# Attention and a gated feed-forward layer on one core: three score banks as one PSUM tile, one maximum pass over two banks, and eight bias rows on ScalarE

## The chip, the cores and the metric

The kernel runs on one core of one Trainium2 chip. The metric is the device time of one execution in microseconds (us); a time stands for the median of its runs. The engines are TensorE (PE, with its weight loads PEld), VectorE (DVE), ScalarE (ACT), GpSimd (POOL), and SyncE (SP), which issues most of the DMAs.

## What is computed

```python
def _attn_ref(q, k, v, s):                    # q, k, v: 8 x 8 x 576 x 64, s: 8 x 8 x 576
    scores = scale * np.matmul(q, k.transpose(0, 1, 3, 2))
    causal = np.triu(np.ones((S, S), dtype=bool), k=1)
    cum = np.cumsum(np.maximum(s, 0.0), axis=-1)
    bias = -(cum[:, :, :, None] - cum[:, :, None, :])
    scores = np.where(causal, -1000000000.0, scores + np.minimum(bias, 0.0))
    scores = scores - np.max(scores, axis=-1, keepdims=True)
    attn = np.exp(scores)
    attn = attn / (np.sum(attn, axis=-1, keepdims=True) + 1e-09)
    return np.matmul(attn, v).astype(np.float32)

def _moe_ref(x, w_gate, w_val, w_out):        # x: 4608 x 512, d_ff = 1536
    gate = 1.0 / (1.0 + np.exp(-(x @ w_gate)))
    val = x @ w_val
    return (gate * val @ w_out).astype(np.float32)
```

The attention's output, with its heads side by side, is the x of the feed-forward part. The bias of a score is a row term, which a softmax takes no notice of, and a column term, the cumulated s; so the kernel adds one row of 576 values per head to all score rows.

## The kernel before

There are 64 heads, numbered through: batch 0 has heads 0 to 7, batch 1 heads 8 to 15. The 576 query rows of a head are cut into five tiles (`TILES`): tile 0 has 64 rows and 64 columns, tile t of 1 to 4 has 128 rows and 64 + 128 t columns, so the longest, tile 4, has 576 columns and the others 448, 320, 192 and 64. A head's tiles are done from 4 down to 0, one in each tick of the main loop, five ticks a head.

A tile goes through these steps. PE makes its scores in PSUM (`n_s` for batch 0 in fp32, `s_part` from head 8 on with operands split into fp16 high and low parts, lines 446 and 447). A PSUM bank holds 512 fp32 values of a partition, so tile 4 is made in two pieces of 288 columns in two banks. GpSimd masks the diagonal block of the bias row in place (`mask_part`, line 461). VectorE adds the bias row to the scores, writes the sum to SBUF and takes the row's extreme in the same instruction (`n_max`, line 584, and `max_part`, line 471), followed by a short instruction that reads the accumulator out. For tile 4 there are two such pairs, and the second starts from the first's result `em`. ScalarE then takes the exponential with that extreme as its bias (lines 587 and 474). The bias row `rl` of a head from 8 on is the head's cumulated row `cr`, spread over all partitions by GpSimd, times a factor of the pair of heads in `qkcf`; `bias_row` makes it on VectorE (line 455). Batch 0 takes the row as it is.

The score pieces take PSUM banks in turn: `score_bank` hands out two buffers of the tag "s" and one of the tag "x", every third piece the latter. A head has six pieces, so tile 4 always lies in the two "s" banks, tile 3 in "x", tiles 2 and 1 in the "s" banks and tile 0 in "x".

Behind the exponentials, `p_part` splits the probabilities into two fp16 parts, DMAs transpose them (`pt`), `av_part` multiplies them with v on PE, and `split_x` and another DMA put the pair's columns into x. The feed-forward part runs in groups of 256 rows: `ffn_in` (line 657, PSUM tile `gv`) has 24 matmuls for each of 12 slices of the hidden width, `ffn_mid` splits the hidden values (lines 672 and 673), `ffn_out` (line 687, PSUM tile `o`) has 6 matmuls of 512 columns a slice. One such slice of a group is called a unit. Groups 0 and 1, 24 units, need the x of batch 0 alone and start while batch 1's attention runs; group 2 needs rows of batch 1. Weights come in as fp32 and are split on ScalarE and VectorE during the first 12 heads.

The order of each engine's queue is not the order of the code: a scheduler lays it out when the kernel is built, by the dependencies, by priorities (`tc.high_priority` in `first`) and by its own estimate of when things are ready. A new PSUM buffer is handed out when the last reader of the old one is done. So an edit can move instructions everywhere.

## Time and profile before

| | before |
|---|---|
| median of 3 runs | 1154.72 us (1151.44 to 1156.39) |
| span of the profiled execution, first to last instruction | 1146.4 us |
| PE busy | 1091.6 us |
| VectorE busy | 776.1 us |
| ScalarE busy | 749.5 us |
| mean granted TensorE clock | 0.985 |

The profile is one execution, taken by itself. It begins with its first and ends with its last instruction; what a run's time has beyond that span is not in it. A row for a group of instructions names the line, the engine, the operation and the tiles (output <- inputs, without buffer numbers), then shapes, the count, the busy time in us, the mean duration of one in ns, and the engine's idle time ahead of them with what ended it. A row of the windows gives, for a stretch of the span, busy us and instruction counts by engine, the granted clock of TensorE, the mean busy share of the 16 DMA engines, and GB/s. In the rows of the slices a digit is the busy share of a fortieth of the span in tenths. A timeline row begins with start and duration in us.

### The profile page before, as it was taken

How to read it: one execution, taken by the hardware profiler on the slowest of the kernel's cores; microseconds unless marked ns; L12 is line 12 of the kernel's file. 1: busy time of each engine (PE TensorE's matmuls, PEld its weight loads, DVE VectorE, ACT ScalarE, POOL GpSimd, SP SyncE). 2: the span in 40 equal slices, each digit the busy share in tenths (PEclk: the TensorE clock that was granted, in tenths of full speed). 3: DMA queues.
4: the chain of work that ended last, by engine and by line, in shares of the span. 5: the costliest groups of instructions: out<-in, count | busy, mean ns of one | idle time of the engine just before them, and what ended most of it. 6: DMA issues, size and time to landing. Idle time of an engine off the chain costs nothing.

```text
span 1146.4 us, 30336 instructions
## 1 busy us (share of the span) xinstructions
PE 1091.6 (95%) x11644; PEld 853.5 (74%) x11644; DVE 776.1 (68%) x2395; ACT 749.5 (65%) x1465; POOL 261.3 (23%) x568
## 2 busy tenths in 40 slices
PE   6787888989999999999999999999999999999998
PEld 4566676658767887788777777778877887787775
DVE  6899999866787777776565677777777775222222
ACT  6989778667777777676665577767776764233222
POOL 6634233222232222121211122212222221000000
PEclk9889899999999999999999999999999999999999
DMA  9676868995989888777646498868887774000000
GB/s 280 201 217 161 185 139 181 183 189 130 171 164 175 164 178 167 141 150 138 145 79 139 89 178 166 166 144 171 156 161 138 150 124 88 13 20 20 1 19 19
DMA packets 445518, 157.62 MB, mean 137 GB/s; under 512 B 403583, under 2 KB 435839, under 8 KB 445374
## 3 DMA queue, kind: packets, MB, share of 16 engines
q1 hardware_dynamic: 418686, 127.38, 57.6%
q10 hardware_dynamic: 23328, 17.04, 4.9%
q0 software_dynamic: 3360, 11.27, 3.0%
q8 instruction: 91, 1.49, 0.5%
q14 instruction: 53, 0.43, 0.1%
HBM read 56.92 MB, written 9.58 MB: 58 GB/s over the span
## 4 chain that ended last, share of the span: by engine, by line
PE 76%; DMA 7%; DVE 5%; issue 5%; ACT 5%; SPq 1%; POOL 1%; ACTq 0%; DVEq 0%; POOLq 0%
PE gv L657 42%; PE o L687 22%; PE s L447 3%; PE s L446 3%; DMA qk<-in_q_dram 1%; PE av L506 1%; PE av L508 1%; PE av L507 1%; DMA v<-in_v_dram 1%; DVE e L471 1%; PE s L575 1%; DMA pt<-p 1%; DMA T<-T 1%; PE na_ps L605 1%; DMA nqk<-in_q_dram 1%
## 5 line engine op out<-in xcount | busy, mean ns | idle before, releaser
L657 PE MATMUL gv<-x,w 128*128 128x256 f16 (+3 forms) x6912 | 613.2, 246 | 5.3 <-DVE t2f L664 2.7
L657 PEld LDWEIGHTS <-w 128*128 128x128 f16 x6912 | 533.8, 98 | 61.5 <-issue 5.2
L687 PE MATMUL o<-w2all,h 128*128 128x512 f16 x1296 | 314.8, 379 | 0.0
L461 POOL TENSOR_SCALAR_AFFINE_SELECT rl<-rl 128x64 f32<-128x64 f32 (+1 forms) x280 | 111.5, 399 | 519.7 <-DVE em L471 465.3
L474 ACT ACTIVATE e<-e,em 128x576 f32<-128x576 f32 x280 | 154.6, 554 | 92.3 <-DVE em L471 90.2
L687 PEld LDWEIGHTS <-h 128*128 128x128 f16 x1296 | 123.6, 98 | 108.7 <-issue 2.4
L662 ACT ACTIVATE th<-gv,scb 128x256 f32<-128x256 f32 (+3 forms) x288 | 111.4, 412 | 139.3 <-PE gv L657 138.4
L664 DVE SCALAR_TENSOR_TENSOR t<-th,gv 128x256 f32<-128x256 f32 x192 | 80.2, 417 | 133.5 <-ACT th L662 132.5
L471 DVE CUSTOM_DVE_ANT_0 e<-s,rl,qkcf 128x288 f32<-128x288 f32 x280 | 135.8, 485 | 30.5 <-PE s L447 24.9
L672 ACT ACTIVATE h<-t,hsc 128x256 f16<-128x256 f32 x192 | 96.6, 503 | 80.0 <-DVE t L664 80.0
L483 DVE SCALAR_TENSOR_TENSOR p<-e,p 128x384 f16<-128x384 f32 x224 | 102.0, 495 | 40.2 <-ACT p L478 39.4
L673 DVE SCALAR_TENSOR_TENSOR h<-t,hsc,h 128x256 f16<-128x256 f32 x192 | 93.2, 486 | 43.3 <-ACT h L672 42.8
L478 ACT ACTIVATE p<-e 128x1152 f16<-128x1152 f32 x112 | 112.1, 1001 | 2.8
L506 PE MATMUL av<-v,pt 128*128 128x65 f16 x560 | 68.0, 193 | 6.9 <-DMA pt<-p 6.9
L507 PE MATMUL av<-v,pt 128*128 128x64 f16 x560 | 68.0, 192 | 0.0
L446 PE MATMUL s<-T 128*128 128x288 f16 (+2 forms) x246 | 64.6, 280 | 3.6 <-DMA T<-qk 2.6
L508 PE MATMUL av<-v,pt 128*128 128x65 f16 x560 | 67.9, 194 | 0.0
L447 PE MATMUL s<-T 128*128 128x288 f16 (+2 forms) x246 | 62.2, 282 | 2.4 <-DMA T<-T 2.4
L506 PEld LDWEIGHTS <-pt 128*128 128x128 f16 x560 | 52.4, 97 | 13.6 <-DMA pt<-p 8.8
L706 POOL DMA_DIRECT2D out_dram<-osb x34 | 19.4, 570 | 174.6 <-ACT osb L705 173.8
L409 POOL PARTITION_BROADCAST cr<-cr x63 | 57.5, 913 | 6.1 <-DVE em L584 5.7
L455 DVE TENSOR_SCALAR rl<-cr,qkcf 128x576 f32<-128x576 f32 x56 | 29.1, 520 | 40.1 <-POOL cr L409 39.9
(157 smaller groups left out, 1436.9 us busy)
## 6 DMA issues: line engine op xcount, KB each, us to landing
v<-v SPq DMA_DIRECT2D x56, 162.5 KB
out_dram<-osb POOLq DMA_DIRECT2D x34, 256.0 KB, 2.9
v<-in_v_dram SPq DMA_DIRECT2D x64, 128.0 KB
T<-T SPq DMA_DIRECT2D x82, 72.0 KB
t2f<-in_v_dram SPq DMA_DIRECT2D x20, 288.0 KB
qk<-in_q_dram SPq DMA_DIRECT2D x17, 288.0 KB
qk<-in_k_dram SPq DMA_DIRECT2D x17, 288.0 KB
w2all<-in_moe_w_gate_dram ACTq DMA_DIRECT2D x7, 512.0 KB
```

The costliest lines, as they stand in the source:

```text
L446: nc.tensor.matmul(ps[:, : b_ - a], lhs, T[i][:, 0, a:b_], start=True, stop=False)
L447: nc.tensor.matmul(ps[:, : b_ - a], lhs, T[i][:, 2, a:b_], start=False, stop=True)
L461: nc.gpsimd.affine_select(rl[i][:, q0:w], rl[i][:, q0:w], pattern=[[-1, m]], compare_op=ALU.is_ge, fill=-MASKED if i < NN else MASKED, bas ...
L471: nc.vector.tensor_tensor_reduce(e_t[t][:, a:b_], ps[:, : b_ - a], rl[i][:, a:b_], c, init, ALU.add, ALU.min, acc)
L474: nc.scalar.activation(e_t[t][:, :w], e_t[t][:, :w], AF.Exp, bias=init, scale=-1.0)
L478: nc.scalar.activation(p_s[h_][:, 0], e_s[h_], AF.Copy, scale=PSCALE)
L483: nc.vector.scalar_tensor_tensor(flat[:, LOW[t] * P : (LOW[t] + t) * P], e_t[t][:, : t * P], PSCALE, flat[:, kb * P : (kb + t) * P], ALU.m ...
L506: nc.tensor.matmul(AV[i][:, t], hi, v_[:, D : 2 * D + 1], start=kb == 0, stop=False)
L657: nc.tensor.matmul(ps[:, gv, a:e], w1[f][:, cc, gv, wl], x_of(b, cc)[:, xl, c0 + a : c0 + e], start=(c == 0), stop=(c == 3 * NC - 1))
L662: nc.scalar.activation(th[:, a:e], ps[:, 0, a:e], AF.Tanh, scale=scb[b][:, f : f + 1])
L672: nc.scalar.activation(h[:, 0], t2, AF.Copy, scale=hsc[:, f : f + 1])
L687: nc.tensor.matmul(ps[:m], h[:, hl, tt * P : tt * P + m], w2[f][:, wl], start=(f == 0 and c == 0), stop=(f == NF - 1 and c == 2))
```

## The change

The three score banks become one PSUM tile `banks` of 3 x 512 columns that lives through the whole kernel; the table `BANK` gives each tile its bank, the same ones as before in effect. The dependencies between score matmuls and maximum passes are now those of the banks within this tile. Tile 4's two pieces lie in banks 0 and 1, and one instruction reads both as a 2 x 288 pattern, adds 576 values of the bias row and takes one extreme; so a head has five such pairs of instructions in place of six. The exponential takes its bias from that one result. The bias rows of heads 8 to 15 are made by ScalarE with a scaled copy, those of heads 16 to 63 by VectorE as before.

```diff
-    score = {"n": 0}
-
-    def score_bank(name):
-        score["n"] += 1
-        tag, bufs = ("x", 1) if score["n"] % 3 == 0 else ("s", 2)
-        return pp.tile([P, 512], F32, tag=tag, name=name, bufs=bufs)
+    banks = pp.tile([P, 3, 512], F32, tag="s", name="score_banks", bufs=1)
+    BANK = {4: 0, 3: 2, 2: 0, 1: 1, 0: 2}
+
+    def halves(x):
+        return x.rearrange("p (a n) -> p a n", a=2)
...
         for a, b_ in pieces:
-            ps = score_bank(f"s{i}_{t}_{a}")
+            ps = banks[:, BANK[t] + (a > 0)]
             nc.tensor.matmul(ps[:, : b_ - a], lhs, T[i][:, 0, a:b_], start=True, stop=False)
             nc.tensor.matmul(ps[:, : b_ - a], lhs, T[i][:, 2, a:b_], start=False, stop=True)
-            S_ps[i, t].append((ps, a, b_))
...
         r = wp.tile([P, S], F32, tag="rl", name=f"rl{i}")
-        nc.vector.tensor_scalar(r, crow[i], qkc[i // 2][1][:, 0:1], None, ALU.mult)
+        factor = qkc[i // 2][1][:, 0:1]
+        if i < 2 * H:
+            nc.scalar.activation(r, crow[i], AF.Copy, scale=factor)
+        else:
+            nc.vector.tensor_scalar(r, crow[i], factor, None, ALU.mult)
         rl[i] = r
...
-        init = MASKED
-        for n, (ps, a, b_) in enumerate(S_ps.pop((i, t))):
-            acc = wp.tile([P, 1], F32, tag=f"em{n}", name=f"em{i}_{t}_{n}", bufs=3)
-            nc.vector.tensor_tensor_reduce(e_t[t][:, a:b_], ps[:, : b_ - a], rl[i][:, a:b_], c, init,
-                                           ALU.add, ALU.min, acc)
-            init = acc
-        nc.scalar.activation(e_t[t][:, :w], e_t[t][:, :w], AF.Exp, bias=init, scale=-1.0)
+        acc = wp.tile([P, 1], F32, tag="em", name=f"em{i}_{t}", bufs=3)
+        r, e = rl[i][:, :w], e_t[t][:, :w]
+        if w > 512:
+            ps, r, e = banks[:, BANK[t] : BANK[t] + 2, : w // 2], halves(r), halves(e)
+        else:
+            ps = banks[:, BANK[t], :w]
+        nc.vector.tensor_tensor_reduce(e, ps, r, c, MASKED, ALU.add, ALU.min, acc)
+        nc.scalar.activation(e_t[t][:, :w], e_t[t][:, :w], AF.Exp, bias=acc, scale=-1.0)
```

`n_s` and `n_max`, the same steps for batch 0, change in the same way.

The first place where the built order shows it is VectorE's queue about the longest tile of head 12. In names, `em12_4` is the extreme of head 12's tile 4, `s12_4_0` and `s12_4_288` its two score pieces, `rl12` the bias row, `t2f` and `h` belong to the feed-forward part, `wa` to the weights, `p16` to the probabilities of the head before; ISA is the pass and the readout behind it. Before:

```order
L471 ISA e_1_80,em12_4_0_2856<-s12_4_0_2816,rl12_2814,qkcf6_2679 128x288
L471 ISA em12_4_0_2856 128x1
L664 SCALAR_TENSOR_TENSOR t2f_135<-th0_11_1849,gv0_11_1824 128x256
L275 SCALAR_TENSOR_TENSOR wa0_137<-ws0_136,wa0_137 128x1024
L483 SCALAR_TENSOR_TENSOR p16_0_81<-e_0_79,p16_0_81 128x128
L483 SCALAR_TENSOR_TENSOR p16_0_81<-e_0_79,p16_0_81 128x256
L491 SCALAR_TENSOR_TENSOR p16_0_81<-e_0_79,p16_0_81 128x2x64
L491 SCALAR_TENSOR_TENSOR p16_0_81<-e_0_79,p16_0_81 128x64
L471 ISA e_1_80,em12_4_1_2858<-s12_4_288_2819,rl12_2814,em12_4_0_2856,qkcf6_2679 128x288
L471 ISA em12_4_1_2858 128x1
```

And in the changed kernel, whose lines are numbered a few higher or lower:

```order
L374 RECIPROCAL qkcf7_2857<-qkcf7_2857 128x1
L673 SCALAR_TENSOR_TENSOR h0_2_2324<-t2f_136,hsc_113,h0_2_2324 128x256
L673 SCALAR_TENSOR_TENSOR h0_3_2333<-t2f_136,hsc_113,h0_3_2333 128x256
L475 ISA e_1_81,em12_4_2758<-score_banks_66,rl12_2719,qkcf6_2592 128x576
L475 ISA em12_4_2758 128x1
L485 SCALAR_TENSOR_TENSOR p16_0_82<-e_0_80,p16_0_82 128x128
```

The two passes and two readouts, which other work stood between, are one pair; and at this head VectorE has already come to the hidden values of units 2 and 3 of group 0 (`h0_2`, `h0_3`), while before it was still at the last `t2f` of group 0 (`th0_11`).

The second place is ScalarE's queue of the changed kernel about head 12's bias row. `th` and `gv` are the feed-forward's, `jq7` are squares of the next pair's q and k, and `e_1` with `em11` are the exponentials of head 11:

```order
L662 ACTIVATE th0_11_1772<-gv0_11_1747,scb0_1276 128x256
L476 ACTIVATE e_1_81<-e_1_81,em11_4_2629 128x576
L356 ACTIVATE jq7_0_2835,ssq1_108<-qk32_7_2807 96x768
L454 ACTIVATE rl12_2719<-cr12_2608,qkcf6_2592 128x576
L662 ACTIVATE th1_0_1883<-gv1_0_1858,scb0_1276 128x256
L356 ACTIVATE jq7_1_2837,ssq1_108<-qk32_7_2807 96x768
L286 ACTIVATE w2all_79,wss17_1849<-wa0_138 128x1024
L476 ACTIVATE e_1_81<-e_1_81,em11_3_2686 128x448
```

The row stands four places ahead of the exponential of head 11's second tile; before, it stood on VectorE, just behind the maximum of that tile.

The third place is PE's queue about the first scores of head 16 (`T16` are its split and transposed q and k; `pt1_15` and `av15` are the probabilities and products of head 15; `gv` and `o` are the feed-forward's PSUM tiles). Before:

```order
L657 MATMUL gv1_9_2293<-x3_133,w1_9_75 128x256
L446 LDWEIGHTS T16_3279
L446 MATMUL s16_3_0_3428<-T16_3279 128x448
L657 LDWEIGHTS w1_9_75
L657 MATMUL gv1_9_2293<-x3_133,w1_9_75 128x256
L657 LDWEIGHTS w1_9_75
L657 MATMUL gv1_9_2293<-x3_133,w1_9_75 128x256
L687 LDWEIGHTS h0_8_2462
L687 MATMUL o0_0_2391<-w2all_78,h0_8_2462 128x512
```

In the changed kernel:

```order
L445 LDWEIGHTS T16_3158
L445 MATMUL score_banks_66<-T16_3158 128x288
L444 LDWEIGHTS T16_3158
L444 MATMUL score_banks_66<-T16_3158 128x448
L445 LDWEIGHTS T16_3158
L445 MATMUL score_banks_66<-T16_3158 128x448
L508 LDWEIGHTS pt1_15_3256
L508 MATMUL av15_3450<-v16_7_3003,pt1_15_3256 128x65
L509 LDWEIGHTS pt1_15_3256
L509 MATMUL av15_3450<-v16_7_3003,pt1_15_3256 128x64
```

Before, head 16's scores stand among units 9 of group 1 and 8 of group 0's output. Now no feed-forward matmul stands between them and the scores of head 17; all matmuls of groups 0 and 1 stand ahead. Counted over the whole queue, there are before the first score of head 16 494 matmuls gv and 48 o in the order before, and 618 and 144 in the changed one; before the first score of head 18 they are 634 and 126, and 672 and 144.

## The prediction

> **What bounds the kernel now.** I read the page first, the parts on busy time and on the slices.

> ```profile
> span 1146.4 us, 30336 instructions
> PE 1091.6 (95%) x11644; PEld 853.5 (74%) x11644; DVE 776.1 (68%) x2395; ACT 749.5 (65%) x1465; POOL 261.3 (23%) x568
> PE   6787888989999999999999999999999999999998
> DVE  6899999866787777776565677777777775222222
> ```

> VectorE (DVE), which the change relieves, is full only in the first eight slices; from the tenth on TensorE (PE) is. So the windows next, cut where the first score matmul of heads 8, 10, 16, 18 and 22 starts (rows below).

> ```profile
> core 0: us, PE busy (x) PEld busy (x) DVE busy (x) ACT busy (x) POOL busy (x), PEclk, DMA share, GB/s
> 0.00:114.10 114.10, 85.96 (x496) 66.26 (x496) 96.11 (x243) 97.61 (x186) 58.58 (x109) 0.89 0.77 216
> 114.10:145.40 31.30, 25.97 (x229) 21.25 (x228) 27.98 (x77) 22.65 (x39) 8.20 (x16) 0.86 0.84 179
> 145.40:221.60 76.20, 67.71 (x718) 53.87 (x719) 68.12 (x223) 61.80 (x116) 26.72 (x49) 1.00 0.83 170
> 221.60:258.50 36.90, 32.99 (x283) 21.75 (x284) 25.64 (x80) 23.81 (x45) 8.23 (x18) 1.00 0.94 179
> 258.50:320.80 62.30, 59.61 (x834) 48.21 (x832) 44.77 (x141) 44.72 (x95) 13.15 (x31) 1.00 0.78 155
> 320.80:964.00 643.20, 641.39 (x7402) 506.31 (x7399) 469.34 (x1532) 447.03 (x876) 143.11 (x341) 1.00 0.75 147
> ```

> After 320.8 us PE lacks 2 us in 643: VectorE time saved there buys nothing. Whatever the change does, it does before 320.8 us, and it counts as PE idle time gained or lost.

> Busy PE overstates its work, since a matmul's row lasts longer than its slot. The slot comes from two timeline rows:

> ```profile
> 195.77 2.46 PE L657 MATMUL gv<-x,w 128*128 128x256 f16 x21
> 254.07 4.48 PE L687 MATMUL o<-w2all,h 128*128 128x512 f16 x20
> ```

> Less the last one's own duration, (2.46 - 0.25) / 20 = 0.11 us per 256 columns and (4.48 - 0.38) / 19 = 0.216 us per 512: 0.43 ns a column. A unit of the feed-forward part is 24 of the first kind (2.65 us) and 6 of the second (1.3 us). A head's attention is 3200 columns of scores and 2585 of products with v: 1.4 + 1.1 = 2.5 us.

> ```profile
> 114.11 0.42 PE L446 MATMUL s<-T 128*128 128x288 f16 x1
> 145.44 0.30 PE L446 MATMUL s<-T 128*128 128x288 f16 x1 [0.57 <-DMA T<-qk]
> 155.40 0.29 PE L446 MATMUL s<-T 128*128 128x288 f16 x1
> 221.56 0.30 PE L446 MATMUL s<-T 128*128 128x288 f16 x1 [0.90 <-DMA T<-qk]
> 258.53 0.29 PE L446 MATMUL s<-T 128*128 128x288 f16 x1
> 320.78 0.29 PE L446 MATMUL s<-T 128*128 128x288 f16 x1
> L657 PE MATMUL gv<-x,w 128*128 128x256 f16 x494 | 61.3, 275 | 3.1 <-DVE t2f L664 2.7 <-ACT x L631 0.4
> L687 PE MATMUL o<-w2all,h 128*128 128x512 f16 x48 | 11.0, 379 | 0.0
> ```

> These are the first scores of heads 8, 10, 11, 16, 18 and 22, and the feed-forward matmuls from head 8 to 16. That stretch holds 494 x 0.11 + 48 x 0.216 = 65 us of feed-forward, eight heads' scores and seven heads' products (19 us) and about 2 us left of batch 0: 86 us of work in 107.5, **21.5 us idle**. Up to head 10 it is 120 matmuls gv (13.3 us) and 5 us of attention in 31.3 us, 13 us idle; the other 8.5 lie behind it. From 16 to 18 some 4 of 37 are idle, from 18 to 22 some 3.5 of 62.

> **The merged pass.** Heads 0 to 7 run through L584, the others through L471.

> From 288 to 448 elements L471 grows by (678 - 512) / 160 = 1.04 ns each, so 576 cost 678 + 133 = 0.81 us, against 0.512 + 0.573; with one readout (0.082) less a head saves **0.36 us**. In L584 it is 0.75 against 0.96, with the readout 0.29. No row shows a pass over two banks. At 1.09 us, the two pieces together, only the readout's 0.08 us would be saved, and dearer it cannot well be, as every element is handled once as before; were it no dearer than 448 columns, 0.49 us. I take the line's value. All 64 heads save 22 us, but those before head 18 only 8 x 0.29 + 10 x 0.36 = 5.9 us.

> [...]

> What waits longer: the third tile's first matmul takes bank 0, which came free after the first piece (0.59 us) and now does after 0.89. Before that third tile is due lie the second tile's mask (0.39, last row) and pass (0.68), so the 0.3 us are covered. Without that cover it is 0.3 us for each of 18 heads, 5 us.

> **The bias rows of heads 8 to 15.**

> ```profile
> L455 DVE TENSOR_SCALAR rl<-cr,qkcf 128x576 f32<-128x576 f32 x56 | 29.1, 520 | 40.1 <-POOL cr L409 39.9
> L474 ACT ACTIVATE e<-e,em 128x576 f32<-128x576 f32 x56 | 43.3, 774 | 53.8 <-DVE em L471 53.6
> L169 ACT ACTIVATE t2f<-t2f 128x576 f32<-128x576 f32 x20 | 13.4, 669 | 0.0
> L478 ACT ACTIVATE p<-e 128x1152 f16<-128x1152 f32 x112 | 112.1, 1001 | 2.8
> POOL rl L461 <- DVE rl L455: 31.9, 48, 1.6
> ```

> VectorE loses 8 x 0.52 = 4.2 us. ScalarE (ACT) gains 8 x 0.77 = 6.2 us by the Exp of the same size with a pointer operand (5.4 by the Square without one). It is busy 84 of 107.5 us between heads 8 and 16, so there is room. The mask on GpSimd (POOL) waits for the row (last line), and the row now stands among exps and copies in ScalarE's in-order queue: a p copy ahead of it makes it some 1 us late, for eight heads 8 us of latency. I count it at nothing, since the row stands ahead of the previous head's last exps and PE has other work meanwhile.

> **What decides is the order.** The scheduler lays all queues out anew. Counted in the order of PE, before head 16's first score stand 494 gv matmuls and 48 o; in the change 618 gv (595 of full width) and 144 o, so all 24 early units. Heads 8 to 16 then hold 595 x 0.11 + 144 x 0.216 + 21 = **117.7 us** of PE work in place of 86. Between heads 16 and 18 the feed-forward shrinks from 28.8 us to 3.1 us: the next group needs batch 1's x, which is not there yet.

> The sum. Heads 0 to 7: ScalarE and VectorE tie at 98 and 96 of 114 us, so 2.8 us less on one is worth between 0 and 2.8; I take 1. Up to head 10 the idle 13 us stay but for the 1.7 us that VectorE (28 of 31 busy) sheds there, less what more feed-forward fills: 11.5. From 10 to 16 I take 4 of the 8.5 idle us, since every score now has up to 16 us of feed-forward ahead and is seldom waited for. Head 16 starts at 114.1 - 1 + 117.7 + 15.5 = 246.3 us (221.6 now). Then two heads alone: the quickest one above took 10.0 us (145.4 to 155.4), heads 8 to 16 on average 13.4; at 11.3 each, with DMA engines at 0.94 there now, head 18 starts at 269. By then 0.9 in-units, 3 out-units and 27 products more are done, 7.0 us of PE work: 262 against 258.5, **3.5 us lost**. Behind it the 3.5 idle us up to head 22 shrink to about 1, since the feed-forward runs ahead again: 2.5 gained. The sum is +1 us on the profiled span of 1146.4. The median of the runs, 1154.7, lies 8.3 us above that span, time that no row of the profile shows and that I carry over. I forecast **no change, 1155.7 us**.

> **The rivals.**

> *Faster.* The new order is the better packing: up to head 10 PE fills 3 us more, from 10 to 16 nothing is idle (-4), and the two heads alone run at 10 us (-2.5). That makes 1155.7 - 9.5, about 1146. For it speaks that VectorE, 96 of 107.5 us busy from head 8 to 16, sheds 7 us there; against it that 13 us of idle time stood before head 10, where PE's order gains only 21 gv matmuls.

> *Slower.* The hole between heads 15 and 18: PE has about 8 us of work there, and heads proceed at what DMA, masks and transposes allow. At 15 us a head (the stretch from 8 to 10 took 15.7) head 18 starts at 276: +7.5, 1163. It decides from 14 us a head. The DMA share of 0.94 at 18 us a head speaks for it, the 10.0 us head against.

> *The clock.*

> ```profile
> 110.00:115.00 5.00, 4.50 (x21) 3.50 (x20) 3.68 (x10) 3.26 (x7) 0.00 (x0) 0.50 0.83 174
> ```

> Where PE is thinly fed before head 9, the granted clock (third number from the end) is 0.50. In the hole that would double 8 us of matmuls; with half of it beside the heads' other waits +4 are left, 1160. [...]

> *The pass doesn't pay*: at 1.09 us the early heads save nothing on it, about +2, 1158.

> **Numbers.** Forecast 0.45, faster rival 0.28, slower rival 0.19, clock 0.05 (at the bound), no saving 0.03. A measurement of this kernel tells about 0.5% (5.8 us) from no change. Faster 0.28, same 0.50, slower 0.22. The range reaches from 1144, the faster rival and 2 us for the larger saving on the pass, to 1165, the slower one and the 2 us of a pass that saves nothing.

> **What would show it.** The merged pass near 0.81 us, the row on ScalarE near 0.77. Head 16's first score at 246 us, head 18's at 269, PE's digits lower in the two slices between and fuller before. PE idle after 320.8 us still about 2 us. I am wrong if head 16 starts before 240 us, if the hole lasts over 28 us, or if PE loses time behind 320 us.

## The result: 6.5% slower, and the profile after

| | before | after |
|---|---|---|
| median of 4 runs | 1153.08 us (1151.18 to 1156.39) | 1226.40 us (1224.49 to 1229.08) |
| ratio, 95% interval | | 1.0645 (1.0608 to 1.0681) |
| span of the profiled execution | 1146.4 us | 1227.3 us |

The forecast of no change was wrong, and the time lies far above its range of 1144 to 1165 us. The spans differ by 80.9 us, the medians by 73.3; a profile is one execution, and the stages below add up to the spans.

The page of the changed kernel, its busy times and slices:

```profile
span 1227.3 us, 30182 instructions
PE 1125.7 (92%) x11644; PEld 870.4 (71%) x11644; DVE 771.8 (63%) x2259; ACT 755.0 (62%) x1473; POOL 264.5 (22%) x568
PE   5778889976989799998999999999899889999998
DVE  6975887656766666668665666677776576522222
```

The instructions that the change touches came out as the rows had promised. These are the groups of the longest tile's pass (heads 8 to 63, then batch 0) and of the bias rows on ScalarE:

```profile
L475 DVE CUSTOM_DVE_ANT_0 e<-score_banks,rl,qkcf 128x576 f32<-128x576 f32 x56 | 45.6, 814 | 21.2 <-PE score_banks L445 20.9
L586 DVE CUSTOM_DVE_ANT_0 e<-score_banks,cr 128x576 f32<-128x576 f32 x8 | 6.0, 753 | 5.6 <-issue 3.1 <-ACT w L291 1.4 <-PE score_banks L576 1.2
L454 ACT ACTIVATE rl<-cr,qkcf 128x576 f32<-128x576 f32 x8 | 6.2, 770 | 3.7 <-POOL cr L408 3.7
```

814, 753 and 770 ns, forecast at 0.81, 0.75 and 0.77 us. What is new stands at the end of the first row: ahead of these 56 passes VectorE waited 20.9 us for score matmuls. So the view of the waits, first before, then after (line and what it waited for, us in total, times, longest):

```profile
DVE e L471 <- PE s L447: 24.9, 44, 2.3
PEld L506 <- DMA pt<-p: 8.8, 7, 2.6
PE av L506 <- DMA pt<-p: 6.9, 7, 2.2
```

```profile
DVE e L475 <- PE score_banks L445: 70.1, 74, 3.0
PEld L508 <- DMA pt<-p: 47.0, 43, 3.0
PE av L508 <- DMA pt<-p: 32.2, 31, 2.8
PE score_banks L444 <- DVE em L475: 19.0, 18, 2.8
```

VectorE waits 70 us for scores in place of 25, and score matmuls on PE wait 19 us for VectorE's extremes. The products `av` come late in turn: PE waits 32 us for transposed probabilities (`pt`) in place of 7, its weight loads 47 in place of 9.

The windows of the changed kernel, cut at the first scores of heads 8, 16, 18, 22 and 63:

```profile
core 0: us, PE busy (x) PEld busy (x) DVE busy (x) ACT busy (x) POOL busy (x), PEclk, DMA share, GB/s
0.00:132.00 132.00, 99.47 (x477) 76.57 (x478) 94.41 (x223) 98.53 (x184) 60.38 (x108) 0.78 0.66 188
132.00:275.10 143.10, 127.86 (x1185) 95.42 (x1185) 106.32 (x310) 104.20 (x193) 34.73 (x70) 0.97 0.72 150
275.10:301.90 26.80, 15.20 (x145) 10.71 (x145) 15.82 (x48) 13.54 (x22) 6.01 (x15) 0.53 0.75 134
301.90:374.30 72.40, 67.21 (x883) 54.19 (x881) 48.84 (x149) 48.91 (x105) 14.93 (x33) 0.98 0.77 149
374.30:1051.00 676.70, 644.03 (x7314) 502.12 (x7312) 459.55 (x1416) 435.39 (x858) 143.82 (x333) 0.99 0.71 138
```

The last row says most. In the stretch where PE had lacked 2 us, it now lacks 33 of 677, while VectorE is busy only 460 and ScalarE 435: no engine beside PE is near full there. Work is waiting for work.

To compare stages with different amounts of feed-forward in them, I take PE's **excess**: the length of a stage, less the columns that its matmuls stream at 0.43 ns each. It holds idle time and time at a lower clock (from 275.3 to 275.8 us of the changed kernel, at a clock of 0.50, score matmuls of 288 columns start 0.24 us apart, against 0.12 at a clock of 1.00), also where a matmul's row, longer than its slot (0.27 us against 0.11 for 256 columns), counts as busy. In batch 0 it holds one thing more: the matmuls there are fp32, and their starts are never closer than 0.84 ns a column (242 ns behind a score matmul of 288 columns), so that some 26 us of the column "to head 8" are streaming time, in the kernel before (26.3) as in the changed one (25.5). The stages are cut at the same first scores in every kernel:

| excess of PE, us | to head 8 | 8 to 16 | 16 to 18 | 18 to 22 | 22 to 63 | rest | sum |
|---|---|---|---|---|---|---|---|
| before | 87.8 | 22.8 | 3.9 | 3.6 | 2.4 | 3.3 | 123.8 |
| after | 106.5 | 25.3 | 19.0 | 7.9 | 42.6 | 3.4 | 204.7 |

The 80.9 us are 18.7 in batch 0, 21.9 between heads 8 and 22, and 40.2 behind head 22, where the prediction had expected neither loss nor gain.

### The profile page after: what moved, and what is told of

Read it like the earlier page. It is cut to its first block, busy times and chain, and to the rows that moved or that the text cites. A ratio compares the mean times of both kernels' runs of the same rounds, so it can differ in the third digit from the quotient of the medians.

```text
span 1227.3 us, 30182 instructions
## 1 busy us (share of the span) xinstructions
PE 1125.7 (92%) x11644; PEld 870.4 (71%) x11644; DVE 771.8 (63%) x2259; ACT 755.0 (62%) x1473; POOL 264.5 (22%) x568
## 4 chain that ended last, share of the span: by engine, by line
PE 53%; DMA 16%; DVE 9%; issue 9%; ACT 9%; POOL 2%; SPq 2%; ACTq 0%; DVEq 0%; POOLq 0%
PE gv L657 28%; PE o L687 14%; DMA pt<-p 9%; DMA v<-in_v_dram 3%; DVE p L485 2%; PE score_banks L444 2%; PE na_ps L605 2%; PE score_banks L445 2%; DVE e L475 2%; PE av L508 1%; ACT jq L356 1%; PE score_banks L576 1%; DMA T<-qk 1%; DMA qk<-in_q_dram 1%; PE nt_ps L596 1%
## 5 line engine op out<-in xcount | busy, mean ns | idle before, releaser
L657 PE MATMUL gv<-x,w 128*128 128x256 f16 (+3 forms) x6912 | 641.0, 248 | 7.4 <-DMA x<-x 5.3
L657 PEld LDWEIGHTS <-w 128*128 128x128 f16 x6912 | 540.4, 99 | 88.0 <-issue 7.7
L687 PE MATMUL o<-w2all,h 128*128 128x512 f16 x1296 | 316.4, 379 | 0.7 <-ACT h L672 0.7
L475 DVE CUSTOM_DVE_ANT_0 e<-score_banks,rl,qkcf 128x576 f32<-128x576 f32 x280 | 152.8, 546 | 74.8 <-PE score_banks L445 70.1
L687 PEld LDWEIGHTS <-h 128*128 128x128 f16 x1296 | 123.2, 98 | 106.5 <-ACT h L672 1.5
L664 DVE SCALAR_TENSOR_TENSOR t<-th,gv 128x256 f32<-128x256 f32 x192 | 79.9, 416 | 126.1 <-ACT th L662 123.8
L508 PE MATMUL av<-v,pt 128*128 128x65 f16 x560 | 74.8, 196 | 35.3 <-DMA pt<-p 32.2
L508 PEld LDWEIGHTS <-pt 128*128 128x128 f16 x560 | 53.4, 99 | 51.5 <-DMA pt<-p 47.0
L444 PE MATMUL score_banks<-T 128*128 128x288 f16 (+2 forms) x246 | 68.4, 284 | 20.3 <-DVE em L475 19.0
L509 PE MATMUL av<-v,pt 128*128 128x64 f16 x560 | 74.3, 195 | 0.0
L510 PE MATMUL av<-v,pt 128*128 128x65 f16 x560 | 73.6, 196 | 0.0
L445 PE MATMUL score_banks<-T 128*128 128x288 f16 (+2 forms) x246 | 68.8, 286 | 0.0
L408 POOL PARTITION_BROADCAST cr<-cr x63 | 62.0, 984 | 8.7 <-DMA cr<-cum_d 8.4
L509 PEld LDWEIGHTS <-pt 128*128 128x128 f16 x560 | 53.9, 99 | 4.7
L510 PEld LDWEIGHTS <-pt 128*128 128x128 f16 x560 | 54.0, 99 | 1.8 <-issue 0.2
```

Source lines behind the costliest of these rows:

```text
L475: nc.vector.tensor_tensor_reduce(e, ps, r, c, MASKED, ALU.add, ALU.min, acc)
L508: nc.tensor.matmul(AV[i][:, t], hi, v_[:, D : 2 * D + 1], start=kb == 0, stop=False)
L509: nc.tensor.matmul(AV[i][:, t, 0:D], hi, v_[:, 0:D], start=False, stop=False)
L510: nc.tensor.matmul(AV[i][:, t], lo, v_[:, D : 2 * D + 1], start=False, stop=False)
L657: nc.tensor.matmul(ps[:, gv, a:e], w1[f][:, cc, gv, wl], x_of(b, cc)[:, xl, c0 + a : c0 + e], start=(c == 0), stop=(c == 3 * NC - 1))
L687: nc.tensor.matmul(ps[:m], h[:, hl, tt * P : tt * P + m], w2[f][:, wl], start=(f == 0 and c == 0), stop=(f == NF - 1 and c == 2))
```

## Where the waits come from

In the built program the waits of each instruction can be read. For one head's tiles, these are the waits of score matmuls and passes for each other, before and after (a pass is VectorE's instruction on a tile):

```
                          before                          after
pass of tile 3            scores of tile 3                scores of tile 2
pass of tile 2            scores of tile 2                scores of tile 1
scores of tile 1          pass of tile 4, second piece    pass of tile 3
scores of tile 0          pass of tile 3                  pass of tile 2
scores of the next 4      passes of tiles 2 and 1         pass of tile 1
```

Before, each pass waits for its own scores, and scores wait for the last reader of their own bank. After, every wait is for the newest instruction on the other side in the code's order, whatever bank it used: the pass of tile 3 reads bank 2, but waits for the scores of tile 2, which write bank 0. Dependencies are taken for the tile as a whole. So scores of tile t wait for the pass of tile t + 2, which waits for the scores of tile t + 1: the two alternate strictly, and a third bank no longer lets scores run ahead.

The timeline shows it. Before, scores of tiles 1 (192 columns) and 0 (64) follow each other, and both passes come later:

```profile
760.42 0.25 PE L446 MATMUL s<-T 128*128 128x192 f16 x1
...
760.61 0.19 PE L447 MATMUL s<-T 128*128 128x64 f16 x1
762.26 0.41 DVE L471 CUSTOM_DVE_ANT_0 e<-s,rl,qkcf 128x192 f32<-128x192 f32 x1
...
763.02 0.28 DVE L471 CUSTOM_DVE_ANT_0 e<-s,rl,qkcf 128x64 f32<-128x64 f32 x1
```

After, one kind stands between two of the other, each pass one tile behind the scores ahead of it:

```profile
853.20 0.25 PE L445 MATMUL score_banks<-t2f 128*128 128x192 f16 x1
854.12 0.54 DVE L475 CUSTOM_DVE_ANT_0 e<-score_banks,rl,qkcf 128x320 f32<-128x320 f32 x1
855.77 0.19 PE L444 MATMUL score_banks<-t2f 128*128 128x64 f16 x1
855.80 0.19 PE L445 MATMUL score_banks<-t2f 128*128 128x64 f16 x1
856.75 0.40 DVE L475 CUSTOM_DVE_ANT_0 e<-score_banks,rl,qkcf 128x192 f32<-128x192 f32 x1
857.93 0.29 PE L444 MATMUL score_banks<-T 128*128 128x288 f16 x1
...
858.30 0.29 PE L445 MATMUL score_banks<-T 128*128 128x288 f16 x1
858.73 0.28 DVE L475 CUSTOM_DVE_ANT_0 e<-score_banks,rl,qkcf 128x64 f32<-128x64 f32 x1 [0.55 <-PE score_banks L445]
```

The last pass, 64 columns of bank 2 whose scores were written at 855.8, has its wait of 0.55 us put down to scores of the next head in banks 0 and 1.

That makes the theory, and three rivals. **The shared tile** (theory A in the expectations): the whole loss is these waits, with what follows from them. **The order**: the loss comes from the new order of PE's queue (144 `o` matmuls ahead of head 16 in place of 48, then a hole), and the waits are its symptom. **The bias rows** (theory C) on ScalarE come late and delay the masks. **The merged pass** (theory B) itself delays the third tile. Theories D and E are told where they come up. All kernels below compute the full reference; a ratio is to the kernel before, run on the same chip.

## Experiments

### The tile alone

The change's one tile, but with two passes for the longest tile and all bias rows on VectorE, as before.

```diff
-        if w > 512:
-            ps, r, e = banks[:, BANK[t] : BANK[t] + 2, : w // 2], halves(r), halves(e)
...
+        for n, (a, b_) in enumerate([(0, w)] if w <= 512 else [(0, w // 2), (w // 2, w)]):
+            ps = banks[:, BANK[t] + n]
...
-            nc.scalar.activation(r, crow[i], AF.Copy, scale=factor)
```

> Three score banks as one tile, but tile 4 still in two passes and all bias rows on VectorE. Theory A (the shared tile: in the built program a pass waits for the newest score matmuls anywhere in the tile and a score matmul for the newest pass anywhere in it, so the two alternate): 1210 to 1235 us, VectorE waiting for score matmuls about 70 us in place of 25. Theory B (the merged pass holds two banks too long): about 1153 us. Theory C (ScalarE's bias rows come late): about 1153 us.

Measured: 1240.7 us, ratio 1.0767 (1.0722 to 1.0813). Its waits:

```profile
DVE e L469 <- PE score_banks L445: 72.3, 81, 6.3
PE av L504 <- DMA pt<-p: 28.8, 27, 5.0
```

The tile alone costs more than the whole change, 6 us above the range expected by theory A, and leaves the same waits. Merged pass and bias rows are not needed for the loss.

### The same banks as three tiles

```diff
-    banks = pp.tile([P, 3, 512], F32, tag="s", name="score_banks", bufs=1)
+    banks = [pp.tile([P, 512], F32, tag=f"s{n}", name=f"score_bank{n}", bufs=1) for n in range(3)]
...
-            ps = banks[:, BANK[t] + n]
+            ps = banks[BANK[t] + n]
```

> Control: the same fixed banks for the whole kernel, but as three tiles of one bank each; two passes, bias rows on VectorE. Theory A: 1153 us within 0.5%, since only a shared tile ties the banks together. Theory D (a bank that is fixed for the whole kernel, in place of buffers handed out in turn, gives the scheduler a worse order): over 1200 us.

Measured: 1152.75 us, ratio 1.0001 (0.9986 to 1.0017).

```profile
DVE e L469 <- PE score_bank L445: 24.6, 42, 2.4
PE av L504 <- DMA pt<-p: 4.9, 5, 2.1
```

The banks and their fixed use are the same as in the run above; only what counts as one tile differs, and with it 7.7%. Its span is 4.8 us longer than that of the kernel before at an equal median: so much differs between two profiles, and smaller differences in the table of excess are not read.

### Two tiles, with the merged pass

Banks 0 and 1 as one tile, so that one pass can read them, bank 2 as another; bias rows on VectorE.

```diff
+    pair = pp.tile([P, 2, 512], F32, tag="s", name="score_pair", bufs=1)
+    third = pp.tile([P, 512], F32, tag="x", name="score_third", bufs=1)
```

> The merged pass, with banks 0 and 1 as one tile and bank 2 as another; bias rows on VectorE. Tiles 2 and 1 of a head still share the first tile with tile 4. Theory A: most of the loss is gone, 1145 to 1165 us; the pass stays at 0.81 us. Theory B: as slow as the change, over 1210 us.

Measured: 1163.97 us, ratio 1.0093 (1.0065 to 1.0122). One bank told apart from the other two removes most of the loss. Tiles 4, 2 and 1 still share a tile, and behind head 22 this kernel still has 9.4 us of excess where the kernel before has 2.4 (table below). The saving of the merged pass doesn't show here either.

### The bias rows alone

The kernel before, with its eight bias rows of heads 8 to 15 on ScalarE.

```diff
+        if i < 2 * H:
+            nc.scalar.activation(r, crow[i], AF.Copy, scale=factor)
+        else:
+            nc.vector.tensor_scalar(r, crow[i], factor, None, ALU.mult)
```

> The kernel before with the bias rows of heads 8 to 15 on ScalarE and nothing else. Theory A: 1148 to 1160 us. Theory C: 20 us or more above before, as the masks of eight heads wait for ScalarE.

Measured: 1161.01 us, ratio 1.0067 (1.0038 to 1.0095). They cost a little by themselves, a tenth of the change's loss; that is 1 us more than theory A had room for, and far from the 20 us of theory C.

### The waits put in, without the shared tile

Three tiles and two passes again, but each score matmul is made to wait for the newest pass and each pass for the newest score matmul.

```diff
+        call()
+        made = [x for x in ins[n:]]
+        if newest[other] is not None:
+            tc.add_manual_dep(made[0], newest[other], SYNC, reason="alternate")
+        newest[kind] = made[-1].name
```

> Three tiles of one bank each, two passes, all bias rows on VectorE: the control, which ran like before. Put in by hand are only the waits that the shared tile brought: a pass waits for the newest score matmul of any bank, and a score matmul for the newest pass of any bank. Theory A (these waits, and the order that follows from them, are the whole loss): 1225 to 1250 us, like the one tile with two passes (1241). Theory E (something else about one tile, such as its place in PSUM): about 1153 us.

Measured: 1243.06 us, ratio 1.0786 (1.0761 to 1.0812).

```profile
DVE e L483 <- PE score_bank L458: 69.1, 85, 4.0
PE av L518 <- DMA pt<-p: 32.8, 27, 3.7
PE score_bank L457 <- DVE em L483: 19.9, 20, 2.1
```

The interval overlaps that of the tile alone (1.0722 to 1.0813), and the waits agree within a few us. With no shared tile, the waits alone make the whole loss of the tile alone; what they make includes the new order of the queues, which came with them.

### The waits taken out, with the shared tile

One tile and the merged pass, bias rows on VectorE; the dependencies are given bank by bank. Each instruction still waits for those that touch its own bank.

```diff
+                if last:
+                    tc.add_manual_dep(x, last[-1], SYNC, reason="same bank")
+            for y, bs in recent[other]:
+                if not set(bs) & set(of):
+                    tc.declare_no_dep(x, y, reason="other bank")
```

> The one tile of three banks and the merged pass, all bias rows on VectorE, but the order is told by bank: a pass waits for the score matmuls of its own banks and a score matmul for the last pass of its own bank. Theory A: 1145 to 1165 us, with VectorE waiting for score matmuls about 25 us. If the merged pass itself is worth something: under 1150. Theory E: over 1210.

Measured: 1157.78 us, ratio 1.0046 (1.0023 to 1.0069).

```profile
DVE e L491 <- PE score_banks L464: 30.0, 36, 4.5
PE av L525 <- DMA pt<-p: 1.6, 2, 1.1
```

This profile is of the fastest of the twelve executions (1151.75 us), so its waits and its row in the table below are those of a good execution, not of the median.

### The change, with the waits taken out

The kernel above with the eight bias rows on ScalarE: the change itself, as the prediction had taken it.

> The change as it stands (merged pass, eight bias rows on ScalarE) with the same waits taken out. Theory A: 1150 to 1170 us; against the run without bias rows on ScalarE it shows what those cost, which alone were 0.67% above before.

Measured: 1161.3 us, ratio 1.0081 (1.0053 to 1.011), against 1.0645 for the change. This is the kernel that I had forecast at 1155.7.

### The change, with its bias rows back on VectorE

> The change with its one tile and merged pass, but all bias rows back on VectorE. Theory A: the loss stays, 1210 to 1240 us. Theory C (the bias rows are the cause): about 1153.

Measured: 1237.3 us, ratio 1.0729 (1.0699 to 1.0758). Its code differs from that of the run at 1.0046 in the waits alone. Against the change, whose rows are on ScalarE, it is about 0.8% slower, while the same move had cost 0.7% in the kernel before. So the price of the eight rows has no fixed sign; it depends on what stands around them.

### Four rows, and sixteen

The kernel before with the rows of heads 12 to 15, and of heads 8 to 23, on ScalarE (`if 12 <= i < 2 * H`, and `if i < 3 * H`).

> The kernel before with four bias rows (heads 12 to 15) on ScalarE; the whole set of eight cost 1.0067 when moved alone. If the loss comes row by row, from the 0.77 us on ScalarE and the mask that waits for a row that comes late, half the rows cost about half: 1.003 to 1.004. If it comes from the order that the scheduler lays out anew (in the run with eight rows 48 matmuls gv stood ahead of head 10's first score in place of 120, and the loss was made before head 22), the four rows give any value between 0.997 and 1.010 that goes with the idle time of PE up to head 22, and not with the number of rows.

> The kernel before with sixteen bias rows (heads 8 to 23) on ScalarE. Row by row: twice the loss of eight, about 1.013. By the order: nothing that follows the number; heads 16 to 23 lie where PE is the bound or near it, so between 0.998 and 1.010, and the loss is again made before head 22.

Measured: 1152.91 us, ratio 1.0010 (0.9992 to 1.0028), and 1160.0 us, ratio 1.0074 (1.0052 to 1.0097). Four rows cost nothing that can be told from noise, eight 0.67%, sixteen 0.74%: not a price a row. What goes with it is the order: ahead of head 10's first score stand 120 `gv` matmuls before and with four rows, and 48 with eight and with sixteen. The loss is made before head 22, as the table shows; it shows the loss too large, since the profile of four rows is of the fastest of its ten executions, and those of eight and of sixteen rows are of the slowest of theirs.

| excess of PE, us | to head 8 | 8 to 16 | 16 to 18 | 18 to 22 | 22 to 63 | gv, o ahead of head 16 |
|---|---|---|---|---|---|---|
| before | 87.8 | 22.8 | 3.9 | 3.6 | 2.4 | 494, 48 |
| four rows | 87.7 | 21.1 | 5.0 | 5.4 | 2.1 | 528, 72 |
| eight rows | 93.5 | 30.3 | 4.0 | 6.5 | 1.7 | 451, 41 |
| sixteen rows | 94.2 | 29.4 | 6.4 | 3.8 | 2.0 | 451, 41 |
| three tiles | 91.0 | 23.9 | 3.4 | 3.8 | 3.2 | 494, 48 |
| two tiles, merged pass | 94.7 | 27.2 | 2.6 | 2.6 | 9.4 | 466, 29 |
| three tiles, waits put in | 106.0 | 34.2 | 17.2 | 6.4 | 50.4 | 618, 144 |
| one tile, two passes | 107.9 | 31.3 | 17.7 | 5.1 | 51.8 | 618, 144 |
| change, rows on VectorE | 103.0 | 32.6 | 18.7 | 8.8 | 45.5 | 618, 144 |
| the same, waits taken out | 87.7 | 28.2 | 2.2 | 4.1 | 1.9 | 507, 22 |
| change | 106.5 | 25.3 | 19.0 | 7.9 | 42.6 | 618, 144 |
| change, waits taken out | 87.1 | 32.9 | 5.8 | 4.7 | 0.6 | 480, 43 |

An order was not held fixed while rows were moved, so this stays the likelier reading and isn't settled; the rows of heads 8 to 11 could have a price of their own that those of heads 12 to 15 have not.

The table also decides between the waits and the order. Every kernel with the alternating waits has 618 and 144 matmuls ahead of head 16, also the one of three tiles to which only the waits were added; none without them has, whether or not its tile is shared. The new order follows from the waits. Why is a reading, not a measurement: the scheduler lays the queues out by its estimate of when scores can start, and with late scores it fits the feed-forward in ahead of them. The hole between heads 16 and 18 (17 to 19 us, against 2 to 6) comes and goes with it. No run has the order without the waits, or the waits without the order; so how the loss divides between the waiting itself and the order laid out around it stays open.

## Why the prediction was wrong, by its steps

**The step that failed** is the one on what waits longer. It took the dependencies to be "those of the banks within this tile", as the section on the change says, looked for one bank that comes free later, and found 0.3 us, covered. In the built program a wait goes to the newest instruction on the tile, so every pass waits for the next tile's scores and no bank matters. Three pairs of runs, in each of which these waits are all that differs in the code, price it at 7.9% (1.0001 to 1.0786), 6.8% (1.0046 to 1.0729) and 5.6% (1.0081 to 1.0645), the order that comes with them included. The built program tells this without a run: I had used it for what stands where in each queue, and not for what each instruction waits for.

**"Whatever the change does, it does before 320.8 us"** failed with it, and was a weak step by itself. Of the three signs of being wrong that the prediction named, this one came true (PE lacks 33 us behind head 22); the other two did not, with head 16 not before 240 us and a hole of under 28 us. That PE lacks 2 us in 643 says that time saved elsewhere buys nothing there. It doesn't say that nothing can be lost: a bound engine stays bound only while its work arrives, and half of the loss (40.2 of 80.9 us) arose there. The view had one direction, and I used it in both.

**The order** was read rightly and given the wrong cause. I took 618 and 144 for a packing that the lighter VectorE allows, and gave 4.5 us of credit between heads 10 and 16 for it, beside 1.5 before head 10 and 1 in batch 0. But it comes with the waits: the tile alone, whose VectorE has no work taken off it, has the same 618 and 144. Head 16's first score came at 275.1 us (forecast 246.3): 19 us of the delay were there at head 8 already (132.1 against 113), the other 10 arose between the heads. The first window above shows that batch 0 paid twice: 477 matmuls had 99.5 us of rows at a clock of 0.78, where before 496 had 86.0 at 0.89.

**The hole** was real and nearly of the forecast size: 26.8 us from head 16 to head 18 against 22.7. That the size came out near is luck. The prediction had heads proceed there at what DMA, masks and transposes allow; the longest waits of PE there are those of scores for passes. The first score of head 16 itself, which writes bank 0, waited for the pass of head 15's tile 1, which had read bank 1; the second row is the sum of such waits in the hole:

```profile
275.15 0.40 PE L444 MATMUL score_banks<-T 128*128 128x288 f16 x1 [2.76 <-DVE em L475]
PE score_banks L444 <- DVE em L475: 9.0, 6, 2.8
```

The clock in the hole was 0.53, as the clock rival had feared: 0.50 from 275.1 to 299 us. What brought it down no run shows. Hole and clock rivals together would have reached 1167 us at most.

**The merged pass** was right as a price: a head saves 0.512 + 0.573 - 0.814 = 0.271 us and one readout, 0.35 us together, against 0.36 forecast. What it buys was forecast at little, 1 us in batch 0 and 1.5 before head 10, and the runs show nothing: where the waits are out, the kernel with the merged pass and all rows on VectorE has a ratio of 1.0046 (1.0023 to 1.0069), a little slower than the kernel before. Even in its fastest execution the excess to head 8 is 87.7 us, as before, and behind head 22 it is 1.9 against 2.4; a gain of 1 us is less than two profiles can tell apart. Why it is slower by 0.46% is not shown. On top of the alternating waits merging makes 1.0767 into 1.0729, and the intervals overlap.

**The bias rows' latency** was counted at nothing. Moved alone they cost 0.67%, and four of them nothing, so the cost does not go by the number of rows, and what makes it is open; and in the change they make it faster (1.0645 against 1.0729).

**The sum** without the failed step would have been 0.7% low, 8 us: the change without the alternating waits has a ratio of 1.0081 (1.0053 to 1.011), which at 1154.7 us is 1164, just inside the range; the forecast's was 1.001. Its profile has that loss between heads 8 and 16: 32.9 us of excess there against 22.8 before, where the forecast had taken 6 us off. The 8.3 us between span and median, which the prediction carried over as time that no row of the profile shows, were a misreading without effect on the forecast: in every execution on record the time is 1.7 to 2.2 us above the span, so most of the 8.3 us says that the profile is of a quick execution.

No version here beats the kernel before.

## What to carry to other kernels

Joining buffers into one tile can join their dependencies: before relying on parts of a tile being independent, read in the built program what each of the instructions waits for, above all which instance, since a wait for the newest writer turns several buffers into one. When the order of a full engine's queue changes a lot after a small edit, look for a wait that the edit added before taking the order for a better packing. And an engine that is 99.7% busy tells where savings are worthless, not where delays are harmless.

## What the runs showed that was not expected

The chain of work that ended last leads away from the cause here. Its lines, by engine, before and after:

```profile
PE 76%; DMA 7%; DVE 5%; issue 5%; ACT 5%; SPq 1%; POOL 1%; ACTq 0%; DVEq 0%; POOLq 0%
```

```profile
PE 53%; DMA 16%; DVE 9%; issue 9%; ACT 9%; POOL 2%; SPq 2%; ACTq 0%; DVEq 0%; POOLq 0%
```

The share of DMA has doubled, most of it transposes of the probabilities (9% of the span, 1% before), though the change touches no DMA. They come behind the exponentials, which come behind the late passes; in the change with the waits taken out PE waits 8.3 us for them in place of 32. In the stretch from head 22 to head 63 VectorE (busy 68%), ScalarE (64%) and the DMA engines (share 0.71, against 0.75 in the like stretch before) are not full, and PE, the fullest, lacks 33 us; each wait is short (over the whole span 74 waits of a pass for scores, 3.0 us at most). Many short waits of two engines for each other were the mark of the false dependency here.
